# Turning the next batch's queries one chunk early, moving the tangent product to the output phase, and computing one chunk's output with plain products

## The chip, the cores and the metric

The kernel runs on one core of one Trainium2 chip. The time is the device time of an execution in microseconds (us). The profile is taken of one further execution; its span is the time from its first to its last instruction, some 2 us shorter than the device time of the same run.

## The reference

Eight batches of linear attention with cosine weights feed a two-layer network with a swish activation whose slope differs per channel.

```python
# attention: batch 8, heads 8, sequence 576, head 64
theta = pi / 2 * pos / S
phi(x) = concat(relu(x) * cos(theta), relu(x) * sin(theta))
kv  = einsum('bhsf,bhsd->bhfd', phi(k), v)
z   = sum_s phi(k)
x   = einsum('bhsf,bhfd->bhsd', phi(q), kv) / (phi(q) . z + 1e-6)
# network: 4608 tokens, 512 -> 2048 -> 512
h   = x @ w_in
g   = h * sigmoid(beta * h)
out = g @ w_out
```

## The kernel before

The 4608 tokens are taken in nine chunks of 512. A chunk has an **h phase** (16 groups of four matmuls of 512 columns, each followed by the activation on ScalarE) and an **output phase**. The attention of batch c+1 is computed beside chunk c.

From chunk 1 on the output phase uses seven half-size products in place of eight. They need sums of g (`g_sums`, on VectorE, in every chunk) and sums of the output weights (`w_sums`, once, in chunk 1). T3 is the same memory as B12, so once the weight sums are done the plain weights are gone.

```python
def g_sums(c, i0, i1):
    ...
    nc.vector.tensor_tensor(s1, A21, A22, op=ALU.add)
    nc.vector.tensor_tensor(s2, s1, A11, op=ALU.subtract)
    nc.vector.tensor_tensor(s4, A12, s2, op=ALU.subtract)
    nc.vector.tensor_tensor(s3, A11, A21, op=ALU.subtract)

def o_fast(c, pr, b_bank):        # one pair of 128 tokens, seven products
    def s_0(): prod(a_ps, g_part(0, 0), B11, True, False); nc.scalar.copy(p1, a_ps)
    def s_1(): prod(b_ps, s_part(S2), T2, True, False)     # writes bank 6 (second pair: 7)
    def s_2(): prod(e_ps, s_part(S1), T1, True, False)
    ...                            # an add on VectorE after most of them
```

The attention of one batch, in the order of its dependencies: relu of q and of k (VectorE), a transpose of q by DMA (`q_turn_dma`, qb to qt), the product of the turned queries with the tangent (`q_tan`, GpSimd, qt to qs), v scaled by cosine and by sine (`v_scale`, VectorE, nine instructions each), the kv products (TensorE) and their copy (`kv_take`, VectorE), the numerators (144 tiny matmuls with as many weight loads, TensorE), three divisions out of PSUM (`x_part`, VectorE), each followed by transposes by DMA into the next chunk's x.

```python
def att_q(b):
    q_relu(b, 0); q_relu(b, 1)
    q_turn_dma(b)                                # one buffer qt
    if b + 1 < B: load_raw(b + 1, "q")

# h phase of chunk c = b - 1, by slot (group of four matmuls)
0: num_rest(), att_q(2), v_scale(2, 0)           # chunk 1 only
1: k_relu(b), load of the next k
2: v_scale(b, 1), load of the next v             # sine; on GpSimd for batch 2
7: q_tan(b, 0)
8: q_tan(b, 1)
12: kv_mm, kv_take
3, 7, 11, 13, 15: g_sums                         # and w_sums at 5 and 9 in chunk 1

# output phase
num_all(0, 6); num_all(1, 0); num_all(2, 4)      # numerators into banks 6, 0, 4
x[0](); x_part(0)                                # x_part(0) frees bank 6
x[1](); x_part(1)                                # x[1] writes bank 6
x[2](); x_part(2)
x[3](); x[4](); x[5](); att_q(b + 1)
y[0](); x[6](); y[1](); y[2](); y[3]()
v_scale(b + 1, 0)                                # cosine of the next batch
y[4](); y[5](); y[6]()

# in chunk 0's output phase
for name in "vkq": load_raw(2, name)
```

## Time and profile before

| | before |
|---|---|
| device time, median | 306.4 us (306.06 to 307.28, 3 runs) |
| span of the profiled run | 304.0 us |
| TensorE / VectorE / ScalarE / GpSimd busy | 91 / 75 / 45 / 27% |
| start to chunk 1 | 50.02 us |
| chunk 1 | 44.67 us |
| chunks 2, 3, 4, 5 | 30.62, 30.61, 30.62, 30.73 us |
| chunks 6, 7, 8 with the tail | 29.87, 26.04, 30.82 us |

A chunk is measured here from its first h matmul to the next chunk's. In the profile a line such as `PE ps L284 <- DVE kv L275: 11.0, 1, 11.0` reads: TensorE, about to run line 284 into ps, stood idle because the kv copy of line 275 on VectorE had not ended; 11.0 us in total, once, longest 11.0. "issue" as the releaser means that the engine stood although nothing that the profile records held it back. The lines that carry the reading of before are in the prediction.

### The profile page before, as it was taken

The page shows a single profiled execution, that of the slowest core. Times are in us where ns is not written, and L with a number is a line of the kernel's source. Part 1 is how long each engine was busy: PE and PEld are TensorE (multiplying, and loading weights), DVE is VectorE, ACT ScalarE, POOL GpSimd, SP SyncE. Part 2 cuts the span into 40 slices and gives each one's busy share as a digit, 9 for nine tenths or more (in the row PEclk, how much of TensorE's full clock was granted, in tenths as well). Part 3 has the DMA queues.
Part 4 walks back from the last instruction along what each step waited for, and adds up shares of the span by engine and source line. Part 5 has one row for each costly group of instructions (what it writes and reads, how often), then busy time and mean ns, then how long its engine had stood idle before and what let it go on. Part 6 is the DMA issues. An engine that isn't in the chain of part 4 may idle for free.

```text
span 304.0 us, 8116 instructions
## 1 busy us (share of the span) xinstructions
PE 275.3 (91%) x3420; PEld 179.6 (59%) x3424; DVE 229.5 (75%) x524; ACT 136.2 (45%) x228; POOL 81.2 (27%) x91
## 2 busy tenths in 40 slices
PE   8799999960699989998999899989998999999993
PEld 7454465430585468546854686458645864784583
DVE  5889884699788978897889778997898624632641
ACT  5787776840003730374038313741274038407700
POOL 1452003842035403460345024502460130000000
PEclk9999999997599999999999999999999999999999
DMA  7999999698059924992499459845910640032023
GB/s 269 380 390 384 388 306 389 174 239 307 8 103 213 348 96 90 207 389 82 81 210 334 144 96 205 308 157 94 169 34 4 87 125 5 2 70 71 0 53 88
DMA packets 50422, 53.96 MB, mean 177 GB/s; under 512 B 31169, under 2 KB 31185, under 8 KB 50385
## 3 DMA queue, kind: packets, MB, share of 16 engines
q1 hardware_dynamic: 47504, 45.82, 51.3%
q0 software_dynamic: 2688, 7.34, 9.9%
q8 instruction: 27, 0.44, 0.6%
q10 hardware_dynamic: 192, 0.27, 0.5%
q14 instruction: 11, 0.08, 0.1%
HBM read 36.71 MB, written 9.44 MB: 152 GB/s over the span
## 4 chain that ended last, share of the span: by engine, by line
PE 58%; DVE 23%; DMA 16%; issue 1%; ACT 1%; SPq 1%; DVEq 0%
PE ps L432 28%; PE ps L369 27%; DMA raw_q<-in_q_dram 11%; DVE vb L218 7%; DMA w_stage<-in_moe_w_in_dram 4%; DVE qb L193 2%; PE ps L263 2%; DVE S L387 1%; DVE S L388 1%; DVE xs L306 1%; PE ps L284 1%; DVE win L115 1%; DVE T L394 1%; DVE T L393 1%; DVE S L386 1%
## 5 line engine op out<-in xcount | busy, mean ns | idle before, releaser
L369 PE MATMUL ps<-xt,win 128*128 128x512 bf16 (+1 forms) x580 | 127.4, 378 | 0.1
L377 ACT ACTIVATE g_t<-ps,beta 128x512 bf16<-128x512 f32 x144 | 98.6, 688 | 58.3 <-PE ps L369 56.2
L369 PEld LDWEIGHTS <-win 128*128 128x128 bf16 x580 | 55.9, 98 | 64.6 <-issue 0.5
L408 POOL DMA_DIRECT2D out_dram<-o_sb x56 | 36.3, 654 | 146.1 <-issue 121.6
L432 PEld LDWEIGHTS <-S 128*128 128x128 bf16 x512 | 50.0, 98 | 9.9 <-issue 3.9
L432 PEld LDWEIGHTS <-g_t 128*128 128x128 bf16 x384 | 37.4, 99 | 9.0 <-issue 3.8
L432 PE MATMUL ps<-wout,g_t 128*128 128x256 bf16 x256 | 34.0, 277 | 0.0
L432 PE MATMUL ps<-T,S 128*128 128x256 bf16 x256 | 30.5, 272 | 3.1 <-DVE xs L306 3.1
L221 POOL TENSOR_TENSOR qs<-qt,tanr 128x1152 bf16<-128x1152 bf16 x12 | 29.5, 2483 | 6.8 <-DMA qt<-qb 6.7
L218 DVE TENSOR_SCALAR vb<-raw_v,sin 128x256 bf16<-128x256 f32 x45 | 30.6, 756 | 0.0
L432 PE MATMUL ps<-wout,S 128*128 128x256 bf16 x256 | 30.6, 273 | 0.0
L386 DVE TENSOR_TENSOR S<-g_t 128x512 bf16<-128x512 bf16 (+1 forms) x40 | 14.7, 367 | 19.6 <-ACT g_t L377 19.4
L464 ACT COPY o_sb<-ps 128x256 f32<-128x256 f32 x16 | 6.0, 372 | 46.9 <-PE ps L432 46.9
L452 ACT COPY p<-ps 128x256 f32<-128x256 f32 x16 | 6.0, 372 | 43.0 <-PE ps L432 43.0
L284 PE MATMUL ps<-kv,qt 64*64 64x65 bf16 x576 | 12.7, 200 | 13.0 <-DVE kv L275 11.0
L306 DVE TENSOR_TENSOR xs<-ps,rden 128x768 bf16<-128x768 f32 (+4 forms) x26 | 22.8, 884 | 0.8
L284 PEld LDWEIGHTS <-qt 64*64 64x64 bf16 x576 | 11.4, 112 | 17.6 <-issue 17.2
L432 PE MATMUL ps<-T,g_t 128*128 128x256 bf16 x128 | 16.6, 272 | 2.9 <-DVE o_sb L468 2.9
L387 DVE TENSOR_TENSOR S<-S,g_t 128x512 bf16<-128x512 bf16 (+1 forms) x40 | 17.0, 425 | 1.4
L193 DVE TENSOR_SCALAR qb<-raw_q 128x1152 bf16<-128x1152 f32 x16 | 14.3, 933 | 4.8 <-DMA raw_q<-in_q_dram 4.7
L388 DVE TENSOR_TENSOR S<-g_t,S 128x512 bf16<-128x512 bf16 (+1 forms) x40 | 16.9, 423 | 1.4
L218 DVE TENSOR_SCALAR vb<-raw_v,cos 128x256 bf16<-128x256 f32 x63 | 17.1, 346 | 0.0
(76 smaller groups left out, 240.4 us busy)
## 6 DMA issues: line engine op xcount, KB each, us to landing
raw_v<-in_v_dram SPq DMA_DIRECT2D x7, 1152.0 KB, 9.5
raw_k<-in_k_dram SPq DMA_DIRECT2D x7, 1152.0 KB, 9.5
raw_q<-in_q_dram SPq DMA_DIRECT2D x7, 1152.0 KB, 7.7
out_dram<-o_sb POOLq DMA_DIRECT2D x56, 128.0 KB, 4.7
w_stage<-in_moe_w_in_dram SPq DMA_DIRECT2D x3, 1024.0 KB, 14.0
w_stage<-in_moe_w_out_dram SPq DMA_DIRECT2D x2, 1024.0 KB, 7.7
w_stage<-in_moe_w_out_dram SPq DMA_DIRECT2D x4, 512.0 KB, 12.1
out_dram<-o_sb SPq DMA_DIRECT2D x14, 128.0 KB, 2.4
```

The lines of the kernel that those rows point to most:

```text
L193: nc.vector.tensor_scalar(dst, src, scalar1=0.0, scalar2=None, op0=ALU.max)
L218: nc.vector.tensor_scalar(o, a, scalar1=t[:, n : n + 1], scalar2=None, op0=ALU.mult)
L221: eng.tensor_tensor(dst.rearrange("q n (g p) -> q n g p", g=2), src.rearrange("q n (g p) -> q n g p", g=2), tanr[:, n0:n1].unsqueeze(2).to ...
L284: nc.tensor.matmul(ps[cols, bank + jj, slot * E : (slot + 1) * E], lhsT=(qt, qs)[cs][rows, jp, n, cols], rhs=kv[rows, g, jp, cs, :], start ...
L306: nc.vector.tensor_tensor(o.rearrange("q j n s d -> q j (n s) d"), nv[:, :, a:z, :, 0:D].rearrange("q j n s d -> q j (n s) d"), rden[:, :, ...
L369: nc.tensor.matmul(ps[:, h_bank(c, jt), blocks.start * 64 : blocks.stop * 64], lhsT=win[jt // 4][:, mi, (jt % 4) * P : (jt % 4 + 1) * P], ...
L377: nc.scalar.activation(gs[c, jt // 4][:, jt % 4], ps[:, h_bank(c, jt)], AF.Silu, scale=beta[:, jt : jt + 1])
L386: nc.vector.tensor_tensor(s1, A21, A22, op=ALU.add)
L387: nc.vector.tensor_tensor(s2, s1, A11, op=ALU.subtract)
L388: nc.vector.tensor_tensor(s4, A12, s2, op=ALU.subtract)
L408: eng.dma_start(out=out_v[bb, n], in_=o_sb[hf * HP : (hf + 1) * HP])
L432: nc.tensor.matmul(dst, lhsT=left(i), rhs=right[:, i], start=start and i == 0, stop=stop and i == JT // 2 - 1, skip_group_check=True)
```

## The change

The intent: chunk 1 is the only chunk where VectorE sets the pace, so its list is cut there. Chunk 1's output goes by plain products, which need no sums; the weight sums move behind the kv copy; q of batch 2 is loaded first. For all chunks, the next batch's queries are relued and turned in the h phase, into a second buffer, so that the tangent product can run in the output phase, where VectorE mostly reads PSUM. The order of the products, of the adds and of the four sums of g is changed so that two products stand before the first that needs bank 6.

```diff
-    qt = one.tile([P, 2, NQ, P], BF16, name="qt")
+    qts = [one.tile([P, 2, NQ, P], BF16, name=f"qt{i}") for i in range(2)]
 ...
         nc.vector.tensor_tensor(s1, A21, A22, op=ALU.add)
+        nc.vector.tensor_tensor(s3, A11, A21, op=ALU.subtract)
         nc.vector.tensor_tensor(s2, s1, A11, op=ALU.subtract)
         nc.vector.tensor_tensor(s4, A12, s2, op=ALU.subtract)
-        nc.vector.tensor_tensor(s3, A11, A21, op=ALU.subtract)
 ...
-            for name in "vkq":
+            for name in "qvk":
                 load_raw(2, name)
 ...
+    def one_unit(slot):                      # chunk 1
+        if slot == 0:    num_rest(); att_q(2); v_half(2, 0)
+        elif slot == 4:  k_all(2)
+        elif slot == 6:  v_half(2, 1)        # sine, on VectorE
+        elif slot == 7:  q_tan(2, 0); q_tan(2, 1)
+        elif slot == 12: kv_all(2)
+        elif slot == 14: att_q(3)
+        elif slot == 18: numerators and x_part of batch 2; q_tan(3, 0); q_tan(3, 1)
+        elif slot == 22: w_sums(0, 4)
+        elif slot == 26: w_sums(4, 8); v_half(3, 0)
+    for slot in range(32):                   # 16 h groups, then 16 plain output groups
+        if slot < 16: h_group(1, slot)
+        else:         o_part(1, (slot - 16) // 4, slot % 4)
+        one_unit(slot)
+
+    for c in range(2, NTC):
 ...
+            if slot == 0 and b < B:
+                k_all(b); v_half(b, 1)
+            if slot == 3 and b + 1 < B:
+                att_q(b + 1)
+            if c == 2 and slot == 5:         # T3 in place, after chunk 1's plain products
+                nc.vector.tensor_tensor(T3, B22, B12, op=ALU.subtract)
 ...
+            for t, bank in enumerate((6, 0, 4)):
+                num_all(b, t, bank)
+            if b + 1 < B:
+                q_tan(b + 1, 0)
+                q_tan(b + 1, 1)
+            x_part(b, 0, 6)
+        for n in (1, 5, 6, 2, 7, 3):
+            x[f"m{n}"]()                     # m6 is the first that writes bank 6
+            if n == 5 and b < B: x_part(b, 1, 0)
+            if n == 6: x["a5"](); x["a6"](); x_part(b, 2, 4)
+        x["a7"](); x["a3"](); y["m1"](); x["m4"](); x["a4"]()
+        for n in (5, 6, 2, 7, 3, 4):
+            y[f"m{n}"]()
+            if n != 2: y[f"a{n}"]()
+            if n == 2 and b + 1 < B: v_half(b + 1, 0)
```

The diff is cut to its core; statements are joined on one line here and there.

## The prediction

> **What bounds the kernel now.** I read the page's busy table first (TensorE 91% busy, VectorE 75%), then the chain of waits that ended last, the table of waits, a table of stretches by stage, and last the timelines of VectorE and GpSimd. The kernel takes nine chunks of 512 tokens. A chunk has an h phase (64 matmuls of 512 columns) and an output phase. From chunk 1 on, the output phase is seven fast products for each of two pairs, 112 matmuls of 256 columns. The attention of the next batch is woven in. The table of stretches (start:end, length, busy of TensorE, its weight loads, VectorE, ScalarE and GpSimd, then clock and DMA) I cut where each chunk's first h matmul starts:
>
> ```profile
> 50.02:94.69 44.67, 31.12 (x426) 20.93 (x425) 36.33 (x73) 14.00 (x24) 16.83 (x17) 0.89 0.66 182
> 94.69:125.31 30.62, 29.07 (x395) 19.38 (x393) 26.41 (x61) 12.49 (x20) 10.29 (x10) 1.00 0.71 185
> 125.31:155.92 30.61, 29.06 (x394) 19.40 (x392) 26.43 (x61) 12.49 (x20) 10.65 (x11) 1.00 0.70 194
> 247.30:273.35 26.05, 26.05 (x178) 17.18 (x176) 11.19 (x30) 12.49 (x20) 2.06 (x4) 1.00 0.18 41
> ```
>
> Chunk 1 takes 44.67 us where chunks 2 to 5 take some 30.65. Only there is TensorE far from full and its clock low (0.89). The table of waits names TensorE's idle time:
>
> ```profile
> PE ps L284 <- DVE kv L275: 11.0, 1, 11.0
> PE ps L432 <- DVE xs L306: 3.1, 4, 1.0
> PE ps L432 <- DVE o_sb L468: 2.9, 5, 0.6
> ```
>
> The first is chunk 1's: the numerator products wait once for the kv copy. The other two recur in each chunk: 0.96 us until the first attention division frees bank 6, and 0.6 us until an output add frees the second pair's bank. The chain through chunk 1 (start, length, what) shows why kv is late:
>
> ```profile
> 40.40 15.40 DMA raw_q<-in_q_dram
> ...
> 55.83 4.32 DVE qb L193 x2
> 60.15 2.36 DVE vb L218 x9
> 62.52 1.27 DVE rk L193
> ...
> 65.37 2.80 DVE T L393
> 68.17 0.02 issue
> 68.19 2.76 DVE T L394
> ...
> 78.10 0.62 DVE kv L275
> ```
>
> Batch 2's q lands at 55.8 because it was queued behind v and k. VectorE, in order, then works 22 us without a gap, with the weight sums ahead of the kv copy.
>
> **What the skill says.** (1) "SBUF — State Buffer", Who interferes with whom: GpSimd and VectorE share a port pair under an exclusive lock; a VectorE instruction with two SBUF inputs, or in a two-port mode, blocks beside a GpSimd instruction that reads SBUF, and one with at most one SBUF input outside those modes does not. The trace agrees. Beside GpSimd's two tangent products, VectorE's sums of 0.42 us take 2.5:
>
> ```profile
> 130.04 4.91 POOL L221 TENSOR_TENSOR qs<-qt,tanr 128x1152 bf16<-128x1152 bf16 x2 [1.17 <-DMA qt<-qb]
> 130.14 2.57 DVE L387 TENSOR_TENSOR S<-S,g_t 128x512 bf16<-128x512 bf16 x1
> 132.74 2.49 DVE L388 TENSOR_TENSOR S<-g_t,S 128x512 bf16<-128x512 bf16 x1
> ```
>
> A product out of PSUM at 8.61 us took an undisturbed 0.63 beside a GpSimd product (8.02 to 9.92). (2) "DMA: Bandwidth & Descriptors", HWDGE ordering: descriptors of a ring are consumed in ring order. v, k and q, issued at 36.8, 37.4 and 40.4, landed in that order. (3) "TensorE: Matmul & The Clock Gate", What's actually happening: the array's clock follows its recent activity. After chunk 1's idle time, 144 numerator matmuls took 2.2 us where they take 1.36 in chunk 3.
>
> **Part by part.** *Chunk 1.* The change loads q first, takes the fast products' sums of g out of this chunk, moves the weight sums behind the kv copy, and pays with plain products. TensorE's work, with an h matmul of 0.2158 us (52 in 11.22): h 64 x 0.2158 = 13.81; numerator rest 0.36; kv products 1.15; numerators 1.36; plain output 64 x 0.2158 = 13.81 (against 112 x 0.109 = 12.2 fast). Sum 30.5 us. Can VectorE keep up? An estimate: the queue before q frees at about 45 us (the transpose ahead landed then), a load of 1.18 MB takes some 3.3 us, so q lands near 48.5, v 52, k 55.8. VectorE: the division ends 52.74, query relu 1.43, cosine scaling 2.36, key relu 1.27, sine scaling 2.4: kv operands ready near 60.3; the kv products are reached at 51.36 + 12 x 0.863 = 61.7. No wait. The tangent product: turned queries land near 62.5, plus 4.9 us is 67.4; the numerators come at 68.05. Tight, but no wait expected. The end of the chunk is less clean: batch 3's query relu waits for its data (66) and for GpSimd (67.4), so its transposes run behind two loads, about 71 to 75.5, then comes the load of q for batch 4 (to 78.6), then the x transposes that chunk 2 needs: landing near 82.5 instead of TensorE's 80.6. I allow 1.9 us. Chunk 1: 44.67 - 30.5 - 1.9 = **12.3 us gained**.
>
> *Chunks 2 to 5, h phase.* The tangent product leaves, so VectorE loses some 4.3 us of blocking (nine sine scalings took 6.74 us in chunk 2 against 2.45 free in chunk 3). It gains the query relu, 1.43. Its list: 0.4 + 1.35 + 2.45 + 1.43 + sums 3 x 1.6 + 2 x 1.1 + kv copy 0.6 = 13.2 us in 15. Hidden before, hidden after: worth nothing by itself.
>
> *Chunks 2 to 5, output phase.* Two products rather than one now stand before bank 6 is needed. Take the first product's start as 0 (141.82 in chunk 3). The division ends at 1.95 as before, the third product could start at 2 x 0.873 = 1.75: wait 0.2 in place of 0.96. But VectorE then does division 1 (to 3.3), and the two adds (to 4.1); product m7 needs the second add and could start at 3.7: wait 0.4. The cosine scaling still stands between the second pair's adds: 0.6 stays. Sum 1.2 against 1.55: 0.35 us a chunk, 1.4 in four. Chunk 6 has no next batch and gains about 0.4.
>
> *The tangent product's new place.* It may start when the last numerator has read the old tangents, about 141.9. Divisions and output adds read PSUM and one SBUF operand and are not blocked. The last sums of g are. Before:
>
> ```profile
> 141.29 0.29 DVE L386 TENSOR_TENSOR S<-g_t 128x256 bf16<-128x256 bf16 x1 [0.58 <-ACT g_t L377]
> 141.62 0.29 DVE L387 TENSOR_TENSOR S<-S,g_t 128x256 bf16<-128x256 bf16 x1
> 141.94 0.29 DVE L388 TENSOR_TENSOR S<-g_t,S 128x256 bf16<-128x256 bf16 x1
> 142.15 0.28 DVE L389 TENSOR_TENSOR S<-g_t 128x256 bf16<-128x256 bf16 x1
> ```
>
> With the difference that depends on nothing moved to second place, the last sum starts near 142.03. That is within 0.1 us of GpSimd's start: a race.
>
> **Rivals.** (A) GpSimd wins: the last sum waits 2.4 us, the division ends at 4.3, the third product waits 2.55 rather than 0.2, and the chunk ends 2.0 us longer than before; four chunks lose 8. For it: at 130.1 GpSimd took the lock between two dependent sums. Against: a start some 0.1 us later is enough to avoid it. About 40 to 45%. Time: 306.4 - 12.3 - 0.4 + 8 = 301.7. (B) GpSimd comes second: 306.4 - 12.3 - 1.4 - 0.4 = 292.3. (C) Chunk 1's gain is eaten by DMA order, the numerators waiting for tangents or chunk 2 for its x: up to 4 us back on either. Against: the ring is idle from 75.5 in the kernel before. (D) Plain products only add 1.6 us, with the gap hidden elsewhere: the 11.0 us wait on one copy, itself on the one chain, speaks against it.
>
> **Range and chances.** B and A weighted near 0.6 and 0.4 give (0.6 x 292.3 + 0.4 x 301.7) = 296.1; I say **295.5 us**, range **290.5 to 302.5**, its low end chunk 1 without the stall, its high end A with a little of C. Faster by over 2% means under 300.3: nearly all of B and a third of A with a better chunk 1: 0.73. Same 0.24, slower 0.03 (A with both sums blocked in every chunk).
>
> **What would show it.** Chunk 1 from first h matmul to chunk 2's near 32.4 us, TensorE's 11 us wait on kv gone, clock at 1.0 there. In the h phase nine sine scalings at 2.45 us. In the output phases the last sum of g at 0.29 us (B) or 2.5 (A), and TensorE's wait on the division at 0.2 or 2.5. Wrong if chunk 2 starts past 85 us (C), or if the fixed start up to 50 us has moved: I assume it has not.

## The result

The changed kernel took 297.14 us (median of 4 runs, 295.95 to 297.99) where the kernel before took 306.84 in the same rounds (306.06 to 307.35). The ratio is 0.968, with a 95% interval of 0.964 to 0.973: faster. Executions over 1.5% slower than the fastest of the same kernel are left out of the means. A ratio here is the mean time of one kernel's fast runs over the mean of the other's of the same rounds, so it is not quite the ratio of the medians quoted.

The span went from 304.0 to 295.5 us, 8.5 us less, and the chunks account for all of it:

| stretch | before | after | change | predicted |
|---|---|---|---|---|
| start to chunk 1 | 50.02 | 51.10 | +1.08 | 0 |
| chunk 1 | 44.67 | 30.93 | -13.74 | -12.3 |
| chunk 2 | 30.62 | 29.86 | -0.76 | -0.35, or +2.0 if the race is lost |
| chunk 3 | 30.61 | 33.50 | +2.89 | the same |
| chunk 4 | 30.62 | 32.07 | +1.45 | the same |
| chunk 5 | 30.73 | 32.07 | +1.34 | the same |
| chunk 6 | 29.87 | 29.12 | -0.75 | -0.4 |
| chunks 7 and 8 | 56.86 | 56.85 | -0.01 | 0 |

The changed kernel's table of stretches, one line a chunk from chunk 1 to 4 (columns as in the prediction: length, busy of TensorE, weight loads, VectorE, ScalarE, GpSimd, clock, DMA share, GB/s), answers to the lines of before:

```profile
51.10:82.03 30.93, 30.67 (x375) 14.94 (x377) 22.43 (x43) 14.26 (x23) 14.43 (x12) 1.00 1.07 289
82.03:111.89 29.86, 29.19 (x393) 19.50 (x393) 25.25 (x70) 13.07 (x21) 12.58 (x16) 1.00 0.90 213
111.89:145.39 33.50, 30.75 (x394) 20.22 (x392) 24.26 (x61) 12.49 (x20) 9.99 (x11) 0.95 0.70 174
145.39:177.46 32.07, 29.28 (x394) 19.29 (x392) 24.16 (x61) 12.49 (x20) 10.00 (x11) 1.00 0.71 182
```

In chunk 1 TensorE is now busy for 30.67 of 30.93 us, at full clock, and VectorE's list fell from 36.33 to 22.43 us. Chunk 5 is like chunk 4. Chunks 3 to 5 became longer although VectorE has less to do in them: 24.2 us where it had 26.4.

TensorE's waits in the changed kernel:

```profile
PE ps L431 <- DVE xs L306: 4.0, 2, 2.2
PE ps L431 <- issue: 2.4, 2, 2.1
PE ps L431 <- DVE o_sb L479: 2.4, 4, 0.6
```

The 11 us on the kv copy is gone. The wait on the first division, 1.0 us at the longest before, is now 2.2 us, twice. A wait put down to "issue", 2.1 us, is new in the output phase.

Why chunk 1 fits is seen in VectorE's timeline there (start, length, engine, line, operation, and in brackets the idle time before it and what ended that):

```profile
53.74 1.42 DVE L193 TENSOR_SCALAR qb<-raw_q 128x1152 bf16<-128x1152 f32 x2
...
58.70 2.45 DVE L218 TENSOR_SCALAR vb<-raw_v,sin 128x256 bf16<-128x256 f32 x9
64.24 0.70 DVE L275 CAST kv<-ps 128x520 bf16<-128x520 f32 x1 [3.09 <-PE ps L263]
```

The kv copy, which VectorE reached at 78.10 before, is done at 64.9, and now VectorE waits 3.09 us for TensorE rather than the other way round.

Not all of the 22 us before were work. The same two query relus took 4.32 us there (55.83 in the prediction's chain) and 1.42 now, and the first two weight sums 2.80 and 2.76 where the later ones took 0.61 and 0.70. GpSimd was running beside them, with batch 2's sine scaling and then its tangent product, from 65.06 to 70.39. GpSimd's timeline before:

```profile
54.84 4.70 POOL L208 TENSOR_TENSOR vb<-raw_v,sin 128x1152 bf16<-128x1152 f32 x2
```

Some 7 us of VectorE's stretch were thus blocking (2.9 + 2.2 + 2.1). The intent above does not name this, but the change takes it out of the way of the kv copy: the sine scaling goes to VectorE, and the tangent product (61.99 to 66.71) now falls where VectorE waits for TensorE. No run separates this from the shorter list.

Why chunks 3 to 5 lost is seen in VectorE's, GpSimd's and TensorE's timelines at the end of chunk 3's h phase:

```profile
128.29 0.28 DVE L388 TENSOR_TENSOR S<-S,g_t 128x256 bf16<-128x256 bf16 x1
128.61 2.51 DVE L389 TENSOR_TENSOR S<-g_t,S 128x256 bf16<-128x256 bf16 x1
...
131.49 0.96 DVE L306 TENSOR_TENSOR xs<-ps,rden 128x768 bf16<-128x768 f32 x1
```
```profile
128.58 4.77 POOL L221 TENSOR_TENSOR qs<-qt,tanr 128x1152 bf16<-128x1152 bf16 x2 [13.64 <-PE ps L284]
```
```profile
132.50 1.11 PE L431 MATMUL ps<-T,S 128*128 128x256 bf16 x8 [2.17 <-DVE xs L306]
133.41 1.91 PE L431 MATMUL ps<-wout,g_t 128*128 128x256 bf16 x8
135.12 2.71 PE L431 MATMUL ps<-wout,S 128*128 128x256 bf16 x16
```

GpSimd's tangent products start at 128.58, the last sum of g at 128.61, **0.03 us later** (as in chunks 4 and 5: 162.08 and 162.11, 194.15 and 194.18), and the sum takes 2.51 us in place of 0.29. The division behind it ends 2.2 us late, and the third product, which needs the division's bank, waits 2.17 us. After that idle time TensorE also runs at half clock for a while (granted clock 0.50 from 133.4 to 136.7): from the third product's start to the seventh's, the first of the second pair, are 5.16 us (132.50 to 137.66) where chunk 5 takes 3.74, so another 1.4 us are lost. That is what sets chunk 3 apart from chunks 4 and 5.

Chunk 2 shows the same place without the race. Its turned queries came late, so GpSimd could not start before VectorE was through (the two engines' timelines in one):

```profile
98.74 0.29 DVE L389 TENSOR_TENSOR S<-g_t,S 128x256 bf16<-128x256 bf16 x1
101.29 4.73 POOL L221 TENSOR_TENSOR qs<-qt,tanr 128x1152 bf16<-128x1152 bf16 x2 [13.54 <-DMA qt<-qb]
```

### The profile page after: what moved, and what is told of

Same layout as the page of the kernel before. It is cut to its first block, busy times and chain, and to the rows that moved or that the text cites. A ratio compares the mean times of both kernels' runs of the same rounds, so it can differ in the third digit from the quotient of the medians.

```text
span 295.5 us, 7998 instructions
## 1 busy us (share of the span) xinstructions
PE 278.5 (94%) x3369; PEld 175.1 (59%) x3376; DVE 201.4 (68%) x502; ACT 137.0 (46%) x228; POOL 74.9 (25%) x89
## 4 chain that ended last, share of the span: by engine, by line
PE 72%; DVE 13%; DMA 8%; issue 3%; ACT 1%; SPq 1%; DVEq 0%
PE ps L369 39%; PE ps L431 21%; PE ps L412 7%; DMA raw_q<-in_q_dram 5%; DMA raw_v<-in_v_dram 3%; DVE vb L218 3%; DVE S L389 3%; DVE xs L306 2%; PE ps L263 2%; ACT g_t L377 1%; PE ps L284 1%; DVE rden L299 1%; SPq L79 1%; DVE p L473 1%; DVE u L476 1%
## 5 line engine op out<-in xcount | busy, mean ns | idle before, releaser
L407 POOL DMA_DIRECT2D out_dram<-o_sb x56 | 35.1, 632 | 79.3 <-issue 53.1
L431 PEld LDWEIGHTS <-S 128*128 128x128 bf16 x448 | 44.2, 99 | 13.5 <-issue 7.8
L431 PEld LDWEIGHTS <-g_t 128*128 128x128 bf16 x336 | 32.8, 99 | 8.0 <-issue 3.3
L431 PE MATMUL ps<-T,S 128*128 128x256 bf16 x224 | 27.5, 273 | 6.1 <-DVE xs L306 4.0
L431 PE MATMUL ps<-wout,g_t 128*128 128x256 bf16 x224 | 29.9, 278 | 0.2 <-issue 0.2
L412 PE MATMUL ps<-wout,g_t 128*128 128x512 bf16 x121 | 28.3, 379 | 0.6 <-issue 0.3
L431 PE MATMUL ps<-wout,S 128*128 128x256 bf16 x224 | 27.5, 277 | 0.3
L389 DVE TENSOR_TENSOR S<-g_t,S 128x512 bf16<-128x512 bf16 (+1 forms) x35 | 19.7, 562 | 1.2
L412 PEld LDWEIGHTS <-g_t 128*128 128x128 bf16 x128 | 12.1, 98 | 13.7
L486 DVE TENSOR_TENSOR o_sb<-ps,p 128x256 f32<-128x256 f32 x14 | 5.9, 424 | 13.8 <-PE ps L431 13.8
L218 DVE TENSOR_SCALAR vb<-raw_v,sin 128x256 bf16<-128x256 f32 x54 | 14.7, 348 | 0.0
L193 DVE TENSOR_SCALAR qb<-raw_q 128x1152 bf16<-128x1152 f32 x16 | 11.7, 769 | 3.0 <-DMA raw_q<-in_q_dram 3.0
```

Source lines behind the costliest of these rows:

```text
L193: nc.vector.tensor_scalar(dst, src, scalar1=0.0, scalar2=None, op0=ALU.max)
L218: nc.vector.tensor_scalar(o, a, scalar1=t[:, n : n + 1], scalar2=None, op0=ALU.mult)
L407: eng.dma_start(out=out_v[bb, n], in_=o_sb[hf * HP : (hf + 1) * HP])
L412: nc.tensor.matmul(o_ps, lhsT=gs[c, jt // 4][:, jt % 4, tt * P : (tt + 1) * P], rhs=wout[:, jt, :], start=(jt == 0), stop=(jt == JT - 1))
L431: nc.tensor.matmul(dst, lhsT=left(i), rhs=right[:, i], start=start and i == 0, stop=stop and i == JT // 2 - 1, skip_group_check=True)
```

## The experiments

The theory after the result had two parts: the gain is chunk 1's, from its shorter list on VectorE; and what chunks 3 to 5 lost is the race for the SBUF port pair between the last sum of g and the tangent product. The rivals were that the load order earns much of chunk 1's gain or none of it, that the race costs little net because something else holds TensorE anyway, and that the tangent product is better left in the h phase. A third part came with the first four runs: a stall named "issue" lies under the race, and TensorE is then waiting for its own instructions.

Times are medians of the fast runs, with their range; each kernel was correct. Kernels of one batch share the runs of the kernel before, whose medians were 306.97 (first four runs), 307.23 (the next four: q first, fast chunk 1, gate and shift, gate and late load), 306.96 (three runs: order vkq, shift alone, all with shift) and 306.52 (the last).

### Chunk 1's rework alone (e4_chunk1)

The kernel before, with chunk 1 taken from the change (load order, plain products, weight sums late, its `one_unit` with the queries of batch 3 in the output phase, as before); chunks 2 to 8 as before.

```diff
-            for name in "vkq":
+            for name in "qvk":
...
+    for slot in range(32):            # chunk 1: h groups, then plain output groups
+        ...
+        one_unit(slot)                # att_q(3) at slot 20; no q_tan(3)
-    for c in range(1, NTC):
+    for c in range(2, NTC):
```

> The kernel before with chunk 1's rework alone (q first among the loads, plain products, weight sums late; one query buffer; chunks 2 to 8 as before). Theory: chunk 1 takes about 31 us instead of 44.7, chunks 2 to 6 keep 30.6, 30.6, 30.7, 30.7 and 30.0 us: total about 293 us, less than the changed kernel's 297.1, since the second part of the change lost 3.6 us net. Rival (chunk 1's gain needs queries turned in the h phase): more than 297 us.

It took 296.03 us (294.94 to 296.15), ratio 0.963 [0.958, 0.968]. Chunk 1 took 30.83 us, chunks 2 to 4 the 30.62 of before, and chunk 5 33.74, with a 2.24 us "issue" stall that ends at 192.94 and a lower clock (0.95). The line of chunk 5 in the table of stretches:

```profile
173.84:207.58 33.74, 30.68 (x395) 20.40 (x392) 27.89 (x61) 12.49 (x20) 10.25 (x11) 0.95 0.64 171
```

The total is 3 us above the expected 293, and chunk 5 is 3.1 us longer than before: the stall and the clock are the difference. Even so chunk 1 alone earns as much as the whole change (0.963 against 0.968), and all that was done to chunks 2 to 6 came to nothing or slightly less as it stands.

### q first in the kernel before (e5_qfirst)

```diff
-            for name in "vkq":
+            for name in "qvk":
```

> The kernel before with only the order of batch 2's loads changed, q ahead of v and k. Theory: q lands near 48.5 us instead of 55.8, VectorE starts chunk 1's work at 52.7 instead of 55.8 and so ends it some 3 us earlier; chunk 1 falls from 44.7 to about 41.5 us, total about 304 us; the rest of chunk 1's gain is VectorE's list (sums of g and of the weights), which this leaves. Rival (q's late landing is the cause of chunk 1's gap): chunk 1 near 33 us, total about 295.

It took 305.28 us (304.25 to 306.53), ratio 0.993 [0.988, 0.997]. Chunk 1 took 41.98 us in place of 44.67. TensorE still waited 10.72 us for the kv copy: q came earlier, but the list behind it, weight sums included, was as long. GpSimd's blocking only moved: the query relu, ahead of GpSimd's sine scaling (58.33), took 1.42 us here, and the cosine scaling beside it 6.21 in place of 2.44.

### The changed kernel with the old load order (e6_vkq)

```diff
-            for name in "qvk":
+            for name in "vkq":
```

> The changed kernel with batch 2's loads back in the order v, k, q. Theory: q lands near 56 to 57 us instead of about 49, VectorE then has 1.43 + 2.36 + 1.27 + 2.4 us to do and makes the kv operands ready near 64, some 1 us after TensorE asks (63); the turned queries and their tangents come some 3 us later, so the numerators wait up to 3 us: chunk 1 32 to 34 us instead of 30.9, total 298 to 300 us. Rival (with VectorE's list short, the order is hidden): chunk 1 about 31 us, total 297 us.

**This was a miss.** It took 296.36 us (296.31 to 296.54), ratio 0.965 [0.960, 0.970], no slower than the changed kernel. VectorE's query relu waited for q until 56.09, 2.35 us later than with q first, and yet chunk 1 took 30.96 us. VectorE's timeline there:

```profile
56.09 1.43 DVE L193 TENSOR_SCALAR qb<-raw_q 128x1152 bf16<-128x1152 f32 x2 [2.10 <-DMA raw_q<-in_q_dram]
...
64.45 0.70 DVE L275 CAST kv<-ps 128x520 bf16<-128x520 f32 x1 [0.93 <-PE ps L263]
```

The kv copy comes at 64.45 against 64.24, and VectorE still waits for TensorE ahead of it (0.93 us rather than 3.09): with the sums out of the way the list has slack enough to hide a later q. The load order is worth 2.7 us to the long list and nothing to the short one.

### The changed kernel with fast products in chunk 1 (e7_fast1)

The early queries and the load order stay; chunk 1 gets its sums of g and the weight sums back in the h phase and the seven products.

```diff
-    for slot in range(32):
-        if slot < 16:
-            h_group(1, slot)
-        else:
-            o_part(1, (slot - 16) // 4, slot % 4)
-        one_unit(slot)
-    for c in range(2, NTC):
+    for c in range(1, NTC):
...
+            if c == 1 and slot in (5, 9):
+                w_sums(slot - 5, slot - 1)
```

> The changed kernel with chunk 1 back on fast products: the sums of g and of the weights return to chunk 1's h phase, all else kept. Theory: VectorE then has about 22 us of work and some blocking by GpSimd in a 15 us h phase, so the output phase starts 8 to 12 us late against 1.6 us fewer on TensorE: chunk 1 about 38 to 41 us, total 304 to 307 us. Rival (the plain products are not what matters): chunk 1 near 30 us, total 296 us.

It took 304.14 us (303.33 to 307.29; a fourth run, 311.43, was slow), ratio 0.992 [0.986, 0.999]. Chunk 1 took 40.59 us. The sums of the fast products put VectorE behind again, and the tangent product falls onto the sine scalings and blocks them, in VectorE's timeline:

```profile
61.50 6.69 DVE L218 TENSOR_SCALAR vb<-raw_v,sin 128x256 bf16<-128x256 f32 x9
```

The kv copy comes at 74.22, ten microseconds later than with plain products, and TensorE waits 1.85 and 2.13 us on the sine scalings, 2.07 on the kv copy and 1.25 on the division. Plain products, which by the prediction's count cost TensorE 1.6 us more, are what buys most of chunk 1's gain: 40.59 to 30.93 us. The run does not separate the sums of g from the weight sums, which the fast products need early, nor from the 4.2 us of blocking on the sine scalings.

### A nudge of 0.1 us for GpSimd (e1_nudge)

A tiny GpSimd write into qs, which must wait for the same numerators, ahead of the two tangent products. They overwrite what it writes, so the result stays right.

```diff
             if b + 1 < B:
+                nc.gpsimd.memset(qs[:, 0, NQ - 1, 0:2], 0.0)
                 q_tan(b + 1, 0)
```

> One tiny GpSimd write (two zeros in the tangent buffer, where the last numerator read; no values change, the tangent product overwrites them) ahead of the two tangent products of the output phase, so that these start some 0.1 us later. Theory (a race for the shared port): VectorE's last sum of g, which started 0.03 us after GpSimd in chunks 3 to 5 and took 2.5 us, now gets the port first and takes 0.29 us; TensorE's wait on the division (1.9 to 2.2 us) goes; chunks 3 to 5 fall from 33.5, 32.1 and 32.1 to about 29.9 us each, the total from 297.1 to about 289 us. Rival (GpSimd's 4.8 us beside the output phase cost VectorE time wherever they lie, or the new product order makes the wait): a shift of 0.1 us changes nothing, 296 to 298 us.

It took 293.95 us (292.51 to 296.87), ratio 0.958 [0.951, 0.966]. Chunk 3 in VectorE's and GpSimd's timelines:

```profile
128.32 0.29 DVE L389 TENSOR_TENSOR S<-g_t,S 128x256 bf16<-128x256 bf16 x1
```
```profile
128.28 0.10 POOL L747 MEMSET qs<- 128x2 bf16 x1 [13.61 <-PE ps L284]
128.46 4.73 POOL L221 TENSOR_TENSOR qs<-qt,tanr 128x1152 bf16<-128x1152 bf16 x2
```

The tangent product now starts 0.14 us after the sum rather than 0.03 before it, and the sum takes 0.29 us in place of 2.51. The race is confirmed. The time fell by only some 3 us, however (the intervals of the two ratios just overlap), not to the 289 that the race alone would give back: chunks 3, 4 and 5 now show "issue" stalls of TensorE, 1.86, 2.90 and 0.82 us, at the place where it had waited for the division. The rival that something else stands behind the race was partly right.

### A gate in place of a nudge (e2_gate)

A dependency rather than a delay: GpSimd first copies one column of the first division's reciprocal, so it cannot start before VectorE has passed the sums.

```diff
+            got = x_rden(6, 0, 0, 3, (0, 1))
             if b + 1 < B:
+                gate = small.tile([P, 1], FP32, name="gate", tag="gate")
+                nc.gpsimd.tensor_copy(gate, got[1][:, 0, 0, 0:1])
                 q_tan(b + 1, 0)
                 q_tan(b + 1, 1)
-            x_part(b, 0, 6)
+            x_mul(got, 0, 3)
+            x_turn_dma(b, 0, 3)
```

> The tangent products wait for the first division's reciprocal (GpSimd first copies one column of it), which VectorE makes after the last sum of g. Theory: no two-input or two-port VectorE instruction is left beside them (divisions and output adds read PSUM), so the last sum takes 0.29 us in every chunk, the divisions keep 0.96 us and the output adds 0.42, chunks 3 to 5 take 29.9 us, total about 289 us, like the nudge but with no race. Rival (any VectorE work beside GpSimd is slowed): the divisions and adds grow, total 294 us or more.

It took 295.61 us (294.43 to 298.07), ratio 0.964 [0.957, 0.970]. Every last sum took 0.29 us, and the divisions beside GpSimd's product took their usual 0.96. Yet chunks 3 and 4 took 31.27 and 33.66 us. Chunk 4, in VectorE's, GpSimd's and TensorE's timelines:

```profile
159.68 0.29 DVE L389 TENSOR_TENSOR S<-g_t,S 128x256 bf16<-128x256 bf16 x1
```
```profile
160.53 4.71 POOL L221 TENSOR_TENSOR qs<-qt,tanr 128x1152 bf16<-128x1152 bf16 x2
```
```profile
160.37 0.27 PE L431 MATMUL ps<-T,S 128*128 128x256 bf16 x1
163.31 3.13 PE L431 MATMUL ps<-T,S 128*128 128x256 bf16 x15 [2.67 <-issue]
```

TensorE stops after the first matmul of a product all of whose operands were ready at that first one. It stands for 2.67 us, and its next 15 matmuls take 3.13 us, where in the changed kernel 15 such matmuls took 1.84 after a stall.

What it waited for is suggested by the DMA queues in the stretch from 160.75 to 161.00 (packets, MB, share of the 16 engines):

```profile
q8 instruction: 1, 0.02, 22.6%
```

One packet of the instruction queue moves there, 16 KB, and TensorE resumes 2.4 us after its start. Other stalls of this kind (start of the packet and resumption, by the packed traces): 129.45 and 131.85, 160.92 and 163.31, 191.10 and 193.47 (this kernel); 190.81 and 193.24 (nudge); 162.95 and 165.19 (the changed kernel); 190.27 and 192.94 (chunk 1 alone); 170.57 and 172.97 (before, a stall of 0.79). In this kernel the packet moved just as the 1.18 MB load of q ended (the data queue had 98.2% of the engines from 160.25 to 160.75). In its trace 3,500 matmuls and weight loads lie before the stall of chunk 3 and 4,268 before that of chunk 4, 768 apart.

The traces of all fourteen kernels say the same. TensorE has 38 issue stalls of over 0.2 us in them. The count of matmuls and weight loads recorded before such a stall is always 445, 1,204 to 1,207, 1,967 to 1,973, 2,478, 2,739, 3,500 to 3,505, 4,268 to 4,275, 5,034 to 5,041 or 5,809. Within one kernel these counts differ by multiples of 256 to within 10 (some records are missing), although numerators stand there in one kernel and kv, plain or fast products in another. The instruction queue moves 26 or 27 packets of 16 KB for the 6,673 to 6,844 recorded instructions, about 256 each. TensorE resumed 2.2 to 2.7 us after the start of the packet, save three times before chunk 1, where the packet itself took 2.2 to 3.8 us.

The Trainium skill, "Runtime: NRT & Kernel Launch", Instruction fetch mechanics, says that TensorE's instruction memory is a queue refilled in blocks of 16 KB, 256 instructions, by a DMA queue of the sequencer. 768 is three such blocks, and a chunk of the steady part has 784 TensorE instructions by count of the code (three blocks and 16), so the crossings would slide by 16 instructions a chunk. The theory from here: the numerators' 288 instructions run in 1.36 us, more than one block, and the refill that they trigger comes too late when its packet has to stand behind a large load.

### Shifting TensorE's instruction count (e8_gate_shift)

The gate, and 22 warm-up matmuls of 128 columns at the start in place of 58 of 48: about as many columns, 72 instructions fewer with the weight loads, so every later crossing falls elsewhere.

```diff
-    warm_pe(58, 48)
+    warm_pe(22, 128)
```

> The gated kernel with 22 warm-up matmuls of 128 columns in place of 58 of 48 (nearly the same columns, 72 fewer TensorE instructions), which moves the places at which TensorE's instruction stream crosses from one 256-instruction block into the next by 72 instructions. Theory (fetch): in the gated kernel TensorE stood still 1.5 and 2.7 us in chunks 3 and 4 at instruction numbers exactly 3 x 256 apart, until 2.45 us after a 16 KB instruction packet, because 288 short numerator instructions run through a block in 1.4 us; with the crossing some 36 fast matmuls later the packet is there in time, chunks 3 and 4 take 29.9 us, total about 290 us. Rival (a data wait that the profile does not name): no change, 294 to 296 us.

It took 293.65 us (292.75 to 294.40), ratio 0.955 [0.952, 0.959], more than the 290 expected. Chunks 3, 4 and 5 took 29.94, 29.94 and 29.93 us, with no issue stall in any: the stalls went with the instruction count alone. Some of that came back elsewhere. Chunk 1 took 32.36 us (a stall of 0.75 on issue and one of 0.43 on the tangent product), chunk 2 30.65 (a stall of 0.98), and chunk 1 began 1.6 us later than with the gate alone (52.27 against 50.65): in the start, where the gate alone has none, stalls of 1.64 and 0.76 us end at 17.53 and 46.91.

### Moving the load away (e9_gate_qload)

The gate with the old warm-up, and the load of q for batch b+2 issued after the third division rather than in slot 3 of the h phase, so that it does not fill the DMA engines while the numerators run.

```diff
-                att_q(b + 1)
+                att_q(b + 1, False)          # no load here
...
                     x_part(b, 2, 4)
+                    if b + 2 < B:
+                        load_raw(b + 2, "q")
```

> The gated kernel with the next batch's q loaded behind the x transposes of the output phase rather than at the end of the h phase; TensorE's instruction stream is unchanged. Theory (the instruction packet stands behind the 1.18 MB load: in chunks 3 and 4 it moved at 129.4 and 160.9 us, as the load ended): the packets come some 1.5 us earlier or more, the two stalls shrink to about the 0.25 us of chunk 5, total about 290 to 291 us. Rival (only the place of the block crossing matters): stalls as before, 294 to 296 us. A cost may come from x transposes or queries landing later, seen as a wait at a chunk's first h matmul.

It took 291.11 us (290.77 to 292.84), ratio 0.948 [0.945, 0.952]. Chunks 3 and 5 took 29.94 and 29.95 us. Chunk 4 in the table of stretches, where the clock is whole again:

```profile
141.99:172.94 30.95, 29.09 (x394) 19.36 (x392) 22.22 (x61) 12.48 (x20) 10.08 (x12) 1.00 0.78 201
```

Stalls of 1.48, 2.67 and 0.25 us became none, 1.27 and 0.28. So both the place of the crossing and the load in front of the packet matter. In chunk 4 with the gate alone the packet started 2.60 us after the instruction that lies 256 before the stall (158.32 to 160.92), here 0.97 us after it (157.34 to 158.31, by the packed traces); from the packet to the resumption were 2.39 and 2.63 us. The load thus explains some 1.4 to 1.6 us; the 1.27 us that stay came with no such load in front. That the stall is an instruction fetch rests on the packets' times, on the multiples of 256 and on these two runs; the profile itself calls it "issue".

### The shift without the gate (e11_shift)

The changed kernel with the shifted warm-up alone: fetch stalls gone, race left in.

```diff
-    warm_pe(58, 48)
+    warm_pe(22, 128)
```

> The changed kernel, not gated, with only the block crossings moved (22 warm-up matmuls of 128 columns for 58 of 48). Theory: the late instruction packet is gone but the race is still lost, so VectorE's last sum of g takes 2.5 us in chunks 3 to 5 and each takes about 32 us (2.1 us more than the 29.9 with both mended); chunk 1 pays some 1.4 us for crossings moved into it; total about 297 to 299 us. Rival (the fetch was the whole loss): chunks of 29.9 us, total about 293 us.

It took 305.73 us (301.54 to 305.98; a fourth run, 309.10, was slow), ratio 0.991 [0.981, 1.001], and the profiled run is the slow one. **Its total missed the expectation**, so only its waits are used. There was no issue stall in chunks 2 to 5, and the race was lost in all four, chunk 2 included. The line in the table of waits:

```profile
PE ps L431 <- DVE xs L306: 8.7, 4, 2.2
```

Four waits of 2.2 us in place of two: with the fetch stalls out of the way the race stands alone and is lost each time. In this slow profile one chunk took 32.08 us, 1.46 more than before the change; in the other three a drop of the clock came on top, 33.5 us. The start up to chunk 1 took 56.1 us, at a clock of 0.94, with issue stalls of 2.07 and 1.59 us in it, which the theory had not foreseen.

### The tangent product back in the h phase (e3_tan_h)

```diff
+            if slot == 7 and b < B:
+                q_tan(b, 0)
+                q_tan(b, 1)
...
-            if b + 1 < B:
-                q_tan(b + 1, 0)
-                q_tan(b + 1, 1)
...
-            q_tan(3, 0)                # chunk 1
-            q_tan(3, 1)
```

> The tangent products go back to slot 7 of the next h phase, second query buffer kept. Theory: VectorE's list in the h phase is then 13.2 us plus some 4.3 us blocked, 17.5 in 15, so the sums of g and the first division come 2 to 3 us late, chunks 2 to 5 take 31.5 to 33 us, total 296 to 301 us. Rival: the h phase hides the blocking, as it did in the kernel before: chunks of 29.9 us, total about 289 us.

It took 305.88 us (305.24 to 307.31; a fourth run, 311.04, was slow), ratio 0.997 [0.990, 1.004], worse than expected. The profiled run is the slow one, and only its waits are used. GpSimd catches the sine scalings there, since the queries are now turned before it. VectorE's timeline in chunk 3:

```profile
119.98 8.22 DVE L218 TENSOR_SCALAR vb<-raw_v,sin 128x256 bf16<-128x256 f32 x9
```

Nine scalings take 8.22 us in place of 2.45, beside tangent products that run from 121.21 for 4.73, kv comes late (TensorE waits 1.20 us on it in each of three chunks) and issue stalls of 2.2 to 2.8 us follow. So with the queries turned early the tangent product is better out of the h phase: the fast runs lie some 9 us above the changed kernel's. How much of that is the blocking and how much the issue stalls (7.3 us in this profile's output phases, 2.4 in the changed kernel's) no fast trace shows. Before the change TensorE did not wait for VectorE in the h phases of chunks 2 to 5, so there the blocking was hidden.

### Towards a better version (e10_best, e12_final)

From the gate with the late load, the 0.6 us wait that recurs in each chunk on an output add was left. Two moves take it away: product 3 ahead of product 7 in the first pair, and the cosine scaling ahead of the second pair instead of between its adds.

```diff
-        for n in (1, 5, 6, 2, 7, 3):
+        for n in (1, 5, 6, 2, 3, 7):
...
-        x["a7"]()
         x["a3"]()
+        x["a7"]()
+        if b + 1 < B:
+            v_half(b + 1, 0)
...
-            if n == 2 and b + 1 < B:
-                v_half(b + 1, 0)
```

The first try had a shifted warm-up as well, `warm_pe(40, 70)`.

> All that the runs point to: the gate, the q load behind the x transposes, crossings moved by 36 instructions (40 warm-up matmuls of 70 columns), the next cosine scaling moved from between the second pair's adds to behind the first pair's, product m3 ahead of m7. Theory: the 0.59 us wait on an output add and the 0.25 us before m7 go in chunks 2 to 5, which fall from 29.9 to about 29.1 us, the fetch stalls stay away: total about 286 us. Rival (TensorE then finds another wait, such as the tangents running into the scaling): 289 us or more.

It took 294.31 us (293.09 to 295.71), ratio 0.958 [0.952, 0.964], worse than the 291.11 that it was built on. Chunks 2 to 4 took 28.87 us each, as hoped. But the start up to chunk 1 took 55.08 us, and chunk 1 34.9, with a 2.08 us issue stall among the numerators. Moving the crossings by the warm-up had only moved the stall, and the start paid for it a second time, with stalls of 2.57 and 1.18 us.

The last run took the old warm-up back.

> The kernel of e10_best with the warm-up of the changed kernel back (58 matmuls of 48 columns), so the gate, the late q load, m3 ahead of m7 and the moved cosine scaling alone. Theory: the first h matmul of chunk 1 returns from 55.1 to about 50.8 us and chunk 1 to 31.3 us; chunks 2 to 5 keep about 28.9 us, but chunk 4 keeps part of its fetch stall (about 1.3 us) and chunk 5 up to 0.3; total about 287 us, below the 291.1 of the gated kernel with the late load. Rival (the gain of the moved scaling is lost to the fetch stalls): 290 us or more.

It took **286.82 us** (286.19 to 288.31), ratio 0.934 [0.929, 0.939], faster than both kernels. Its chunks 2 to 5 took 28.87, 29.01, 29.76 and 29.44 us; chunk 2 in the table of stretches:

```profile
83.62:112.49 28.87, 28.87 (x393) 19.39 (x393) 23.25 (x64) 12.50 (x20) 10.65 (x12) 1.00 0.81 195
```

TensorE is busy for the whole of chunk 2; 0.82 us of issue stall is left in chunk 4, and 0.63 in chunk 5. Chunk 1 took 33.03 us: the first h matmul of chunk 2 waited 2.03 us, until 83.62, for its x transposes. Their issue ended at 81.97 us here and at 80.37 in the changed kernel, which just escaped that wait: there the second of them landed at 81.89 and the first h matmul started at 82.03, here at 83.48 and 83.62.

### What stays open

What makes a refill late is settled only in part: with no large load in front of its packet the late load still leaves 1.27 us in one chunk, the shift leaves none in three, and both leave or make a stall elsewhere. A different warm-up of about as many columns delays chunk 1 by 1 to 5 us; issue stalls in the start, 2.4 us in one profile and 3.7 and 3.8 in the others, at counts of the list above, go with most of that, and the slow profile has a drop of the clock there besides. The start up to chunk 1 varied from 50.0 to 53.1 us over fast profiles of kernels whose code up to there hardly differs, so 1 us of any total is not explained by the chunks. The x transposes of chunk 2 have no margin: the first h matmul starts 0.14 us after the second of them lands.

## Why the prediction was right, and where its steps were off

The time, 297.14 us, lies inside the range (290.5 to 302.5) and 1.6 us above the point. The mechanisms hold, but several terms were off and some were missing, and the closeness is in part luck: the point lies between two outcomes, 292.3 and 301.7, neither of which came. The race was lost in three chunks of four and cost less than forecast in two of them, and chunk 1's extra 1.44 us were eaten by the start, which took 1.08 us longer. That a moved start would be a sign of being wrong the prediction says itself; why it moved is open.

- **Chunk 1 bounds the gain, and VectorE's list bounds chunk 1: right.** Chunk 1's rework alone gives 296.03 us, and with the fast products put back chunk 1 takes 40.59 us again. The step that was off is the 1.9 us allowed for chunk 2's x: TensorE was idle for 0.26 us in the whole chunk, so the gain was 13.74 instead of 12.3. The sum of TensorE's work, 30.5 us, measured 30.67. The allowance rested on batch 3's query transposes starting at about 71; they were issued at 68.1. That the danger was there is shown by the last run, which did wait 2.03 us. What the account of before left out is the 7 us of blocking by GpSimd in VectorE's 22: the prediction reads the 4.32 us of the query relu and the 2.80 of a weight sum as work, though it counts the same relu at 1.43 after the change.
- **q first is part of the gain: wrong as a cause.** The prediction's list counts it first among what the change does in chunk 1. It is worth 2.7 us with the long list and nothing once the sums are gone.
- **The h phase's lightening is worth nothing by itself: supported.** VectorE's sine scalings went back to 0.35 us each (2.45 for nine), as predicted, and TensorE waits for nothing in the h phases of chunks 2 to 5, before or after. The groups by line, changed kernel (busy, mean ns, idle):

```profile
L218 DVE TENSOR_SCALAR vb<-raw_v,sin 128x256 bf16<-128x256 f32 x54 | 14.7, 348 | 0.0
L389 DVE TENSOR_TENSOR S<-g_t,S 128x256 bf16<-128x256 bf16 x14 | 10.7, 766 | 0.5
```

  The second line is where the blocking went: the mean of the last sums of g, 0.77 us, is a mix of three blocked ones at 2.5 us and eleven at 0.29. Sine scalings had a mean of 756 ns before. The port's blocking was not removed but moved, from the h phase, where it was hidden, to the one sum that the bank's division stands behind.
- **The output phase gains 0.35 us a chunk without the race: right in sign, and more than predicted.** Chunk 2, which escaped the race, gained 0.76, and chunk 6, which has no next batch, 0.75. The step that was off is the sum of the waits. From start to start, the wait for bank 6 had cost 1.13 us before (141.82 to 143.82 for a product of 0.87), not 0.96; of the 0.2 and 0.4 us that were to stay in front of the third and the fifth product (m6, m7), chunk 2 shows none and 0.24 (102.41 where 102.17 was possible), and chunk 6 0.13 and 0.25.
- **The race: right as a mechanism, and nearly a toss-up, as said.** The prediction gave GpSimd 40 to 45%, and put the loss at 2.0 us a chunk. GpSimd won in chunks 3 to 5, by 0.03 us in each; TensorE's wait was 2.17 us in chunk 3 and 1.86 in chunk 5 (2.55 predicted), and the chunks lost 2.89, 1.45 and 1.34 us, the first with the drop of the clock. Chunk 2 escaped, since its turned queries came late; the prediction had all four the same.
- **What was missing.** TensorE's stalls on "issue" were in the profile of before, 0.79 and 0.69 us, and the prediction passed over them. Had VectorE won the race, they would have taken up to 2.9 us a chunk at the same place: the nudge measured 293.95, where rival B with chunk 1's larger gain comes to 292.3 - 1.4 = 290.9. In chunk 4 of the changed kernel the fetch stall and the race ran side by side and only one was paid. The drop of the clock after the 2.17 us idle, 1.4 us in chunk 3, was missing as well.

## What to carry to other kernels

Ahead of moving a GpSimd operation to a "free" stage, look for the last two-input SBUF operation of VectorE that a releasing step stands behind, and tie GpSimd's start to a result that comes after it: a tiny copy of that result does it, while an order that is expected to hold by some 0.1 us may not: here it was lost by 0.03. Where one stage is set by VectorE, plain work on TensorE can be the cheaper form: some 1.6 us more of matmuls here made the chunk 9.7 us shorter. When TensorE stands on "issue" after a burst of tiny matmuls, count the instructions before each stall: where the numbers differ by multiples of 256, look at the instruction queue's packets and at the large load beside them, and move the load before counting on a gain there.

## What the Trainium skill lacked or had wrong

- "Runtime: NRT & Kernel Launch", Instruction fetch mechanics, says that crossing a block boundary is mostly hidden. In these runs TensorE stood for up to 2.9 us (1.48 and 2.67 in the run with the gate) and resumed 2.2 to 2.7 us after the start of the 16 KB packet, after the numerators' 288 instructions in 1.36 us; in the run with the gate the packet moved as a 1.18 MB load ended. Fewer instructions ahead (72 of them) took the stalls from three chunks and put 2.40 us of them into the start, and a later load took one of 1.48 us away whole and one of 2.67 down to 1.27.
- "SBUF — State Buffer", Who interferes with whom, has the exclusive lock right (0.29 us free, 2.5 beside a GpSimd product; a division out of PSUM stayed at 0.96). It says that the order of issue decides who blocks, but nothing of how finely: GpSimd 0.03 us ahead blocked the sum, GpSimd 0.14 us behind did not.
- "TensorE: Matmul & The Clock Gate", What's actually happening, gives an idle window of about 3.4 us, free-running, for the clock to drop. In chunk 3 an idle time of 2.17 us was followed by a clock of 0.76 from 130 to 137 us, which would be 3.4 us at half clock, and cost 1.4 us; in chunks 4 and 5 waits of 2.12 and 1.86 us were not, nor was a stall of 2.90 us in the nudge's run. So a shorter idle time than the page's can do it, and a longer one need not; that this depends on when it falls is not shown.
- No page that was read says what a change of warm-up shape costs: 22 matmuls of 128 columns or 40 of 70 in place of 58 of 48 put chunk 1's start at 52.3 to 56.1 us in three profiles (one of them slow), with 2.4 to 3.8 us of issue stalls in front of it, against 50.4 to 51.3 and no such stall over 0.2 us with the old shape in the fast profiles of the changed kernel and its variants.
